# Weighted sums of the later pairs: both heads in one product over block-diagonal values, one transpose a pair

## The chip, the cores and the metric

The kernel runs on one core of one Trainium2 chip. The metric is device time of one execution in microseconds (us); lower is better. The median of three runs of the kernel before is 865.38 us (864.91 to 868.30).

## The reference

Sparse attention over 8 batches, 8 heads, 576 positions and head width 64, followed by a feed-forward layer with softplus, in 32-bit floats.

```python
scores = scale * np.matmul(q, k.transpose(0, 1, 3, 2))
mask_local = (rel >= 0) & (rel < stride)                                  # heads 0 to 3, stride 32
mask_strided = (rel >= 0) & (pos[None, :] % stride == pos[:, None] % stride)  # heads 4 to 7
attn = softmax(np.where(masks[None, :, :, :], scores, -1000000000.0))
out = np.matmul(attn, v)                         # (8, 8, 576, 64) -> x of 4608 x 512
h = x @ w_in                                     # w_in 512 x 2048
g = np.maximum(h, 0.0) + np.log1p(np.exp(-np.abs(h)))
return (g @ w_out).astype(np.float32)            # w_out 2048 x 512
```

(The softmax line is shortened; the reference writes out maximum, exponential and sum.)

## The kernel before

**Layout.** A *pair* is two heads of one batch; 32 pairs are numbered `n` = 0 to 31, four a batch. Positions of a pair are laid out in 18 blocks of 32 queries (strided heads are re-sorted on the host), and a block sees two blocks of 32 keys: the one before it and its own. For the pairs from 8 on (batch 3 on, 24 pairs), chunk `x` = 0 to 8 stands for two blocks, one in *place* 0 (blocks 0 to 8) and one in *place* 1 (blocks 9 to 17). A chunk's probabilities lie on 128 partitions, `64 * place + 32 * h` and up for head `h`, and in 64 columns, `c` = 0 for the earlier 32 keys and `c` = 1 for the own ones. In chunks 6 to 8 the two heads change places within a place (`place_of`).

**One pair from 8 on.** `head_scores` multiplies queries and keys (36 products of 64 rows and 32 columns, moving 64), VectorE adds the mask (`add_mask`), takes maxima, subtracts, ScalarE takes exponentials, VectorE sums and normalizes. Then `turn` transposes 32 by 32 blocks on VectorE in three tasks, `P{n}.0`, `P{n}.1` and `P{n}`: one whole transpose of 128 partitions and 576 columns (L550), then two transposes of 32 partitions by 288 columns that bring the own keys of the lower 32 partitions up (L555), and two that bring the earlier keys of the upper 32 partitions down (L557). After them the 64 keys of one head lie on the 64 partitions of a place. `late_sums` (L574) then multiplies: for each chunk, place and head one product of 64 rows (keys), 64 columns (the head's values) and 32 moving queries, into half the partitions of one of two PSUM banks, `po` for place 0 and `pv` for place 1. That is 36 products a pair. Each 32-bit product leaves two records of a weight load and two of a product in the trace, 72 a pair.

**Values.** `load_v` fetches `v_late`: on 64 partitions a place, the two key blocks of each chunk with both heads side by side (rows of 512 B). Each value is loaded twice. Three transfers a pair: 32 partitions for the first own block (L320) and 64 partitions a place (L329). For pair 8 GpSimd first zeroes 32 partitions (L318), the block before the first.

**The feed-forward part.** The rest is two kinds of large products, 128 by 128 by 512: `hidden` (L774) and `output` (L843), three products each for a split into a high and a low part, and in the later chunks `product` (L946). One takes its turn behind the other on TensorE, and between them stand, every three steps, the scores of pair `n + 1` and the sums of pair `n` as one task (`S{n+1}`, function `scores_of`). ScalarE and VectorE work out softplus and the splits between.

**What sets the order.** Everything up to the load of pair 8's values and the first products of chunk 1 follows the list `FIRST`, written by hand. After that `Plan` simulates engines with given costs and due times and emits tasks by their planned start; the three transposes of a pair stand in it with costs of 0.80, 0.95 and 0.95. The engines' queues keep the emitted order. Loads and stores are issued from SyncE (SP).

**Memory.** `home_0` to `home_3` are fixed tiles used piecewise: in `home_0` lie `v_late`, `qT` and `mask_late`; in `home_1` the probabilities, `turned` (the transposed ones) and, for pairs 4 to 7, their values `v_in`.

Of the kernel before, what the change touches and what calls it, by code (L numbers as in the profile page):

```python
# [11 lines left out]
BF16 = mybir.dt.bfloat16  # L12
# [6 lines left out]
P = 128  # L19
# [57 lines left out]
class Plan:  # L77
# [8 lines left out]
    def add(self, name, urgency, engine, cost, fn, after=(), late=0.0):  # L86
        self.tasks[name] = (urgency, len(self.tasks), engine, cost, fn, after, late)
# [29 lines left out]
def attention_softplus_ffn(  # L117
# [9 lines left out]
    nc = tc.nc  # L127
    B, NPAIR, _, _, S = qk.shape
    D = P // 2
# [6 lines left out]
    NCHK = NTILE * 3 // 2  # L136
# [30 lines left out]
    homes = [home(k, n, f"home_{k}") for k, n in enumerate(HOMES)]  # L167
# [39 lines left out]
        early[part, PAIRS[-1]][:, lo : lo + 4 * TILE].rearrange("p (h a c) -> p h a c", h=2, a=2)  # L207
        for part, lo in (("l", PAD + S), ("l", PAD + S + 4 * TILE), ("h", 2 * S))
    ]
    mask_late = homes[0][:, 3 * S : 3 * S + NCHK * 32].bitcast(BF16)  # L210
    v_late = homes[0][:, : 2 * S].rearrange("p (x d) -> p x d", d=2 * D)
    turned = homes[1][:, 2 * S : 3 * S].rearrange("p (c x l) -> p c x l", c=2, l=32)
    qT = homes[0][:, 2 * S : 3 * S]
    kT = [homes[2][:, i * (PAD + S) : (i + 1) * (PAD + S)] for i in range(2)]
    v_in = homes[1][:, 2 * S : 2 * S + 2 * NTILE * D]
    prob_all = homes[1][:, : 2 * S]
# [54 lines left out]
    def prob_of(n):  # L271
        if n < NPAIR:
            chunks = prob_early[n][:, PAD:].rearrange("p (a c) -> p a c", c=3 * PAD)
            return chunks[:, :, :64]
        return prob[n % 2]
# [38 lines left out]
    def load_v(n):  # L314
        b, pair = order[n]
        if n >= 2 * NPAIR:
            if n == 2 * NPAIR:
                nc.gpsimd.memset(v_late[:32, 0], 0.0)  # L318
            src = v[b, pair]
            nc.sync.dma_start(v_late[32:64, 0], src[:32])  # L320
            for place in range(2):
                lo = 1 - place
                keys = src[32 * (NCHK * place + lo - 1) :]
                keys = bass.AP(
                    tensor=keys.tensor,
                    offset=keys.offset,
                    ap=[[2 * D, 64], [32 * 2 * D, NCHK - lo], [1, 2 * D]],
                )
                nc.sync.dma_start(v_late[64 * place : 64 * place + 64, lo:], keys)  # L329
            return  # L330
        if n < NPAIR:

            t = room[n]
        else:
            t = v_in
        t = t[:, : 2 * NTILE * D].rearrange("p (a c) -> p a c", c=2 * D)
        src = v[b, pair]
        nc.sync.dma_start(t[PAD:P, 0], src[0:TILE])
        src = src[TILE - PAD : 2 * TILE]
        src = bass.AP(  # L340
            tensor=src.tensor,
            offset=src.offset,
            ap=[src.ap[0], [TILE * 2 * D, NTILE - 1], src.ap[1]],
        )
        nc.sync.dma_start(t[:, 1:NTILE], src)
        vs[n] = t.rearrange("p a (h d) -> p a h d", d=D)
# [52 lines left out]
        if n == 0:  # L399
            add(False)  # L400

    def place_of(part, h):

        return 1 - h if part == 1 else h

    def head_scores(n):

        taken.append(n)
        pss[n, 0] = ps_s.tile([P, 512], F32, tag="ps", name=f"ps_{n}")
        shared[n] = ps_o.tile([P, 512], F32, tag="po", name=f"po_{n}")  # L410
        pss[n, 1] = shared[n][:, S // 2 :]
        for x in range(6):
            for chunk in (x, x + 3) if x > 2 else (x,):
                part = chunk // 6
                for place in range(2):
                    a, i = block_at(chunk, place) if n < 2 * NPAIR else (3 * place, chunk)
                    c = TILE * a + 32 * i
                    for h in range(2):
                        to = 64 * place + 32 * place_of(part, h)
                        head = slice(64 * h, 64 * h + 64)  # L420
                        at = 64 * (chunk - SPLIT[part][0])
                        nc.tensor.matmul(  # L422
                            pss[n, part][to : to + 32, at : at + 64],
                            lhsT=qT[head, c : c + 32],
                            rhs=k_of(n)[head, c : c + 64],
                            start=True,
                            stop=True,
                        )
# [114 lines left out]
                            src[:, lo:hi, 32 * c : 32 * c + 32],  # L543
                        )

    def turn(n, step):

        src = prob_of(n).rearrange("p x (c l) -> p c x l", l=32)
        if step == 0:
            nc.vector.transpose(turned, src)  # L550
            return
        for place in range(2):
            lower, upper = (slice(at, at + 32) for at in (64 * place, 64 * place + 32))
            if step == 1:
                nc.vector.transpose(turned[upper, 0], src[lower, 1])  # L555
            else:
                nc.vector.transpose(turned[lower, 1], src[upper, 0])  # L557

    def late_sums(n, joint):

        if joint:
            to = [shared[n + 1], ps_h.tile([P, 512], F32, tag="ph", name=f"pv_{n}_1")]
        else:
            taken.append(n)
            to = [
                ps_o.tile([P, 512], F32, tag="po", name=f"pv_{n}_0"),
                ps_s.tile([P, 512], F32, tag="ps", name=f"pv_{n}_1"),
            ]
        pos[n, 0], pos[n, 1] = to
        for x in range(NCHK):  # L570
            for place in range(2):
                rows = slice(64 * place, 64 * place + 64)
                for h in range(2):
                    nc.tensor.matmul(  # L574
                        to[place][64 * h : 64 * h + 64, 32 * x : 32 * x + 32],
                        lhsT=v_late[rows, x, D * h : D * h + D],
                        rhs=turned[rows, place_of(x // 6, h), x],
                        start=True,
                        stop=True,
                    )  # L580

    def early_transposes(n, g):
# [128 lines left out]
    part = {}  # L711
# [474 lines left out]
    add = plan.add  # L1186
# [18 lines left out]
    for i in range(begin, len(steps)):  # L1205
        c, f = steps[i]
        w, x = CH[c] / 384, when[i]
        after = [f"F{i-1}", f"u{i-2}", f"G{c}.{f}"] + lows_of(c)
# [3 lines left out]
        after = [f"F{i}", f"Us{i-2}" if f"Us{i-2}" in plan.tasks else f"l{i-2}"]  # L1212
# [4 lines left out]
        else:  # L1217
            after = [f"u{i}", f"O{i-3}"]
            add(f"h{i}", x + 4.1, "ACT", 0.65, lambda c=c, f=f: g_high(c, f, nc.scalar), after)
            after = [f"h{i}", f"O{i-3}"]  # L1220
            fn = lambda c=c, f=f: g_low(c, f, nc.vector)
# [4 lines left out]
        c, f = steps[k]  # L1226
        w = CH[c] / 384
        x = when[i] + 2.1 * w
# [5 lines left out]
        for t in range(nt):  # L1234
            name = f"O{k}" if t == nt - 1 else f"O{k}.{t}"
            after = [f"l{k}", before] + ([f"y{k-1}.{t}"] if f == 0 else [])
            add(name, x + 0.01 * t, "PE", 0.7, lambda c=c, f=f, t=t: output(c, f, (t,)), after)
            before = name
            if f == NFC - 1:
                e, cost, engine = (("ACT", 0.5, nc.scalar), ("DVE", 0.6, nc.vector))[t % 2]  # L1240
                fn = lambda c=c, t=t, engine=engine: result(c, t, engine)
# [4 lines left out]
    for c in range(2, NEAR):  # L1246
        for f in range(10 if c > 2 else 12, NFC):
            old = NFC * c + f - 2 if f > 11 else NFC * (c - 1) + f + 4
            after = [f"F{old}", f"Wt{f}", f"Wt{f-2}"]
# [8 lines left out]
    def scores_of(n, x, y, name, e, cost, after, also=None):  # L1258

        z = x - 11.0  # L1260
        if n > 2 * NPAIR:
            add(f"Q{n}", z, "ACT", 1.4, lambda n=n: lay_out_q(n), [f"q{n}", f"S{n-1}"])

        def work():
            head_scores(n)
            if also is not None:
                sums_of(also)

        add(name, x, e, cost, work, after)
        for j in range(2):  # L1270
            fn = lambda j=j: add_mask(n, j)
            add(f"Y{n}{j}", y + j, "DVE", 0.47, fn, [f"S{n}", f"P{n-2}"])
        after = [f"Y{n}0", f"Y{n}1"]
        for j, (letter, e, cost, fn) in enumerate(
            (
                ("x", "DVE", 0.75, row_maxima),
                ("s", "DVE", 0.75, row_subtract),
                ("E", "ACT", 0.7, row_exp),
                ("z", "DVE", 0.75, row_sums),
                ("g", "DVE", 0.16, lambda n: guard(n, nc.vector)),  # L1280
                ("R", "DVE", 0.2, reciprocals),
                ("M", "DVE", 0.75, lambda n: normalize(n, nc.vector)),
            )
        ):
            add(f"{letter}{n}", y + 1.5 + j, e, cost, lambda fn=fn: fn(n), after)
            after = [f"{letter}{n}"]
        for j, (name, step, cost) in enumerate(
            ((f"P{n}.0", 0, 0.8), (f"P{n}.1", 1, 0.95), (f"P{n}", 2, 0.95))
        ):
            fn = lambda step=step: turn(n, step)  # L1290
            add(name, y + 8.5 + 0.9 * j, "DVE", cost, fn, after)
            after = [name]
        if n + 2 < len(order):
            add(f"k{n+2}", x + 5, "SP", 0.8, lambda: load_k(n + 2), [f"S{n}"], 2.0)
            add(f"q{n+2}", x + 18, "SP", 0.8, lambda: load_q(n + 2), [f"P{n}"], 2.0)
# [432 lines left out]
```

## Time and profile before

| what | value |
|---|---|
| median of three runs | 865.38 us |
| the profiled execution | 865.32 us |
| its span, first to last instruction | 863.5 us |
| granted TensorE clock | 1.000 |
| ScalarE busy | 494.2 us (57%) |
| GpSimd busy | 66.4 us (8%) |

The profile page lists busy time by engine, a row by slices of the span, the chain of work that ended last, and groups of instructions by line. PE is TensorE's products, PEld its weight loads, DVE is VectorE, ACT ScalarE, POOL GpSimd, and SPq SyncE's queue that issues DMAs. L574 is line 574 of the kernel. In a row of instructions, `64*64 64x32` is a product of 64 rows and 64 columns of weights with an output of 64 by 32. A timeline row begins with the start and the duration in us; a row with x2 merges neighbours, and its duration runs from the first start to the last end. The rows that carry the argument stand in the prediction.

### The profile page before, as it was taken

How to read it: one execution, taken by the hardware profiler on the slowest of the kernel's cores; microseconds unless marked ns; L12 is line 12 of the kernel's file. 1: busy time of each engine (PE TensorE's matmuls, PEld its weight loads, DVE VectorE, ACT ScalarE, POOL GpSimd, SP SyncE). 2: the span in 40 equal slices, each digit the busy share in tenths (PEclk: the TensorE clock that was granted, in tenths of full speed). 3: DMA queues.
4: the chain of work that ended last, by engine and by line, in shares of the span. 5: the costliest groups of instructions: out<-in, count | busy, mean ns of one | idle time of the engine just before them, and what ended most of it. 6: DMA issues, size and time to landing. Idle time of an engine off the chain costs nothing.

```text
span 863.5 us, 18656 instructions
## 1 busy us (share of the span) xinstructions
PE 853.9 (99%) x7688; PEld 703.3 (81%) x7688; DVE 584.3 (68%) x1106; ACT 494.2 (57%) x913; POOL 66.4 (8%) x89
## 2 busy tenths in 40 slices
PE   7999999999999999999999999999999999999998
PEld 5787888888888888888888888788888888888886
DVE  7899977677686668776668866666687645656500
ACT  6998755665555555646555655766664355566400
POOL 6345550000000000000000000000000000000000
PEclk9999999999999999999999999999999999999999
DMA  9894215556422554326424543655546144333100
GB/s 325 286 354 152 58 47 195 184 161 217 137 84 90 171 149 130 104 80 200 130 76 149 155 125 118 198 177 187 174 148 209 50 158 135 109 123 122 45 29 24
DMA packets 85332, 124.49 MB, mean 144 GB/s; under 512 B 7296, under 2 KB 52480, under 8 KB 85248
## 3 DMA queue, kind: packets, MB, share of 16 engines
q1 hardware_dynamic: 84960, 122.99, 43.8%
q8 instruction: 60, 0.98, 0.5%
q10 hardware_dynamic: 288, 0.33, 0.1%
q14 instruction: 24, 0.20, 0.1%
HBM read 92.88 MB, written 30.41 MB: 143 GB/s over the span
## 4 chain that ended last, share of the span: by engine, by line
PE 93%; DMA 2%; DVE 2%; ACT 1%; issue 1%; POOL 0%; SPq 0%; ACTq 0%; POOLq 0%
PE py L843 43%; PE ph L774 24%; PE bank_a L946 10%; PE bank_c L946 5%; PE po L574 2%; PE bank_b L946 2%; DMA ro<-in_moe_w_out_dram 2%; PE ps L422 2%; PE py_last L843 1%; PE po L422 1%; PE pv L574 1%; PE pv L640 1%; PE pt L610 1%; DVE home L536 1%; DMA raw_q<-in_qk_dram 0%
## 5 line engine op out<-in xcount | busy, mean ns | idle before, releaser
L843 PE MATMUL py<-w_o,gh 128*128 128x512 f32 x1024 | 318.3, 392 | 0.0
L843 PEld LDWEIGHTS py<-w_o,gh 128*128 128x128 f32 x1024 | 190.4, 188 | 39.5
L774 PE MATMUL ph<-x_h,w_i 128*128 128x512 f32 x656 | 202.7, 390 | 0.5 <-DVE u L798 0.5
L843 PE MATMUL py<-w_o,gl 128*128 128x512 f32 x512 | 199.2, 389 | 0.0
L774 PEld LDWEIGHTS ph<-x_h,w_i 128*128 128x128 f32 x656 | 122.5, 188 | 26.7 <-POOL home L525 0.9
L774 PE MATMUL ph<-x_l,w_i 128*128 128x512 f32 x328 | 127.6, 389 | 0.0
L843 PEld LDWEIGHTS py<-w_o,gl 128*128 128x128 f32 x512 | 96.1, 188 | 20.2
L290 ACT CAST gh<-u 128x512 fp32r<-128x512 f32 x89 | 55.1, 621 | 96.4 <-DVE u L798 74.5
L786 ACT ACTIVATE u<-ph 128x512 f32<-128x512 f32 x84 | 50.2, 599 | 94.8 <-PE ph L774 92.2
L828 DVE TENSOR_TENSOR gl<-u,gh 128x512 fp32r<-128x512 f32 x117 | 80.8, 691 | 25.0 <-ACT gh L290 21.9
L789 ACT ACTIVATE u<-u 128x512 f32<-128x512 f32 x144 | 90.9, 633 | 3.8
L791 ACT ACTIVATE u<-u 128x512 f32<-128x512 f32 x144 | 90.8, 631 | 3.7
L798 DVE SCALAR_TENSOR_TENSOR u<-ph,u 128x512 f32<-128x512 f32 x84 | 57.7, 687 | 37.3 <-ACT u L791 36.6
L774 PEld LDWEIGHTS ph<-x_l,w_i 128*128 128x128 f32 x328 | 61.6, 188 | 13.0
L786 ACT ACTIVATE u<-kept 128x512 f32<-128x512 f32 x45 | 28.5, 633 | 42.4 <-DVE kept L1042 26.0
L290 DVE COPY o<-py 128x512 f32<-128x512 f32 (+1 forms) x15 | 10.0, 670 | 47.0 <-PE py L843 46.8
L481 DVE TENSOR_TENSOR home<-ps,home 128x384 f32<-128x384 f32 x28 | 15.5, 555 | 36.4 <-PE ps L422 34.9
L1042 DVE TENSOR_TENSOR kept<-bank_c,kept 128x512 f32<-128x512 f32 x15 | 10.4, 692 | 36.5 <-PE bank_c L946 35.2
L290 ACT COPY home<-home 128x576 f32<-128x576 f32 x26 | 33.5, 1290 | 1.6 <-DMA home<-in_qk_dram 1.6
L290 ACT COPY o<-py 128x512 f32<-128x512 f32 (+1 forms) x21 | 11.5, 575 | 38.1 <-PE py L843 27.3
L1037 ACT COPY kept<-bank_a 128x512 f32<-128x512 f32 x30 | 17.7, 589 | 25.5 <-PE bank_a L946 24.5
L422 PEld LDWEIGHTS ps<-home,home 64*32 64x32 f32 x1344 | 23.3, 106 | 9.9 <-issue 8.1
(205 smaller groups left out, 1299.5 us busy)
## 6 DMA issues: line engine op xcount, KB each, us to landing
home<-in_qk_dram SPq DMA_DIRECT2D x56, 288.0 KB, 3.5
ws<-far SPq DMA_DIRECT2D x30, 512.0 KB, 3.3
out_dram<-o SPq DMA_DIRECT2D x35, 256.0 KB, 2.3
ri<-in_moe_w_in_dram SPq DMA_DIRECT2D x16, 512.0 KB, 7.3
ro<-in_moe_w_out_dram SPq DMA_DIRECT2D x16, 512.0 KB, 8.3
far_w<-w_i SPq DMA_DIRECT2D x16, 512.0 KB, 4.5
w_i<-far_w SPq DMA_DIRECT2D x16, 512.0 KB, 3.4
near<-far_w SPq DMA_DIRECT2D x15, 512.0 KB, 3.3
```

The lines of the kernel that those rows point to most:

```text
L290: (engine.copy if engine is nc.scalar else engine.tensor_copy)(dst, src)
L422: nc.tensor.matmul(pss[n, part][to : to + 32, at : at + 64], lhsT=qT[head, c : c + 32], rhs=k_of(n)[head, c : c + 64], start=True, stop=True,)
L574: nc.tensor.matmul(to[place][64 * h : 64 * h + 64, 32 * x : 32 * x + 32], lhsT=v_late[rows, x, D * h : D * h + D], rhs=turned[rows, place_ ...
L774: nc.tensor.matmul(ph, lhsT=w_i(c, f)[:, half, cc * P : (cc + 1) * P], rhs=x_at(x, cc, c), start=(i == 0), stop=(i == 3 * NCC - 1),)
L786: nc.scalar.activation(us[c, f], phs[c, f], AF.Abs)
L789: nc.scalar.activation(u, u, AF.Exp, scale=-1.0)
L791: nc.scalar.activation(u, u, AF.Ln, bias=1.0)
L798: nc.vector.scalar_tensor_tensor(to, in0=ph, scalar=0.0, in1=u, op0=ALU.max, op1=ALU.add)
L828: engine.tensor_tensor(g, us.pop((c, f)), ghs[c, f].bitcast(F32), op=ALU.subtract)
L843: nc.tensor.matmul(y_of(c, t), lhsT=g[:, sl], rhs=w32["o", f][:, half], start=(f == ROWS[c][0] and n == 0), stop=(f == ROWS[c][-1] and n = ...
L946: nc.tensor.matmul(bank, lhsT=w_left(p, A, f, half, i), rhs=x_right(p, A, part, i), start=p in "125" and n == 0, stop=n == 5, skip_group_c ...
L1037: nc.scalar.copy(kept(A, s), bank_of(p, A, f))
```

## The change

For the pairs from 8 on, the values are laid out block-diagonally. On the 32 partitions of a place and a head lie that head's values of one key block, in that head's 64 columns, and the other head's 64 columns hold zeros. `v_late` gets ten such blocks of 128 columns (a block more than there are chunks, since chunk `x` takes blocks `x` and `x + 1`). One whole transpose by 32 by 32 blocks leaves the keys `c` of both heads on a place's 64 partitions, and that is now what a product takes: 64 rows (32 keys of head 0, 32 of head 1), 128 columns (both heads), 32 moving queries, and two of them, `c` = 0 and 1, add up. So there are again 36 products a pair: 9 chunks, 2 key blocks, 2 places.

The four transposes of 32 partitions a pair are gone. The heads no longer change places in chunks 6 to 8 of these pairs. Values arrive in four transfers a pair (32 partitions, 9 or 10 rows of 256 B each) without the double copy. The zeros are written once, for pair 8: one fill of 64 partitions and four of 32 partitions by 640 columns. `v_late` grows from 1152 to 1280 columns, so `qT` moves up in `home_0` and `mask_late` moves to `home_1`.

```diff
-    mask_late = homes[0][:, 3 * S : 3 * S + NCHK * 32].bitcast(BF16)
-    v_late = homes[0][:, : 2 * S].rearrange("p (x d) -> p x d", d=2 * D)
+    mask_late = homes[1][:, 3 * S : 3 * S + NCHK * 32].bitcast(BF16)
+    v_late = homes[0][:, : (NCHK + 1) * 2 * D].rearrange("p (x h d) -> p x h d", h=2, d=D)
...
-    qT = homes[0][:, 2 * S : 3 * S]
+    qT = homes[0][:, (NCHK + 1) * 2 * D : (NCHK + 1) * 2 * D + S]
...
-                nc.gpsimd.memset(v_late[:32, 0], 0.0)
-            src = v[b, pair]
-            nc.sync.dma_start(v_late[32:64, 0], src[:32])
+                nc.gpsimd.memset(v_late[:64, 0], 0.0)
+                for quarter in range(4):
+                    rows = slice(32 * quarter, 32 * quarter + 32)
+                    nc.gpsimd.memset(v_late[rows, :, 1 - quarter % 2], 0.0)
+            src = v[b, pair].rearrange("(x l) (h d) -> l x h d", l=32, h=2)
             for place in range(2):
                 lo = 1 - place
...
-                nc.sync.dma_start(v_late[64 * place : 64 * place + 64, lo:], keys)
+                for h in range(2):
+                    rows = slice(64 * place + 32 * h, 64 * place + 32 * h + 32)
+                    keys = src[:, NCHK * place + lo - 1 : NCHK * place + NCHK, h]
+                    nc.sync.dma_start(v_late[rows, lo:, h], keys)
...
-        return 1 - h if part == 1 else h
+        return 1 - h if part == 1 and n < 2 * NPAIR else h
...
-        if step == 0:
-            nc.vector.transpose(turned, src)
-            return
-        for place in range(2):
-            lower, upper = (slice(at, at + 32) for at in (64 * place, 64 * place + 32))
-            if step == 1:
-                nc.vector.transpose(turned[upper, 0], src[lower, 1])
-            else:
-                nc.vector.transpose(turned[lower, 1], src[upper, 0])
+        nc.vector.transpose(turned, prob_of(n).rearrange("p x (c l) -> p c x l", l=32))
...
         for x in range(NCHK):
-            for place in range(2):
-                rows = slice(64 * place, 64 * place + 64)
-                for h in range(2):
+            for c in range(2):
+                for place in range(2):
+                    rows = slice(64 * place, 64 * place + 64)
                     nc.tensor.matmul(
-                        to[place][64 * h : 64 * h + 64, 32 * x : 32 * x + 32],
-                        lhsT=v_late[rows, x, D * h : D * h + D],
-                        rhs=turned[rows, place_of(x // 6, h), x],
-                        start=True,
-                        stop=True,
+                        to[place][:, 32 * x : 32 * x + 32],
+                        lhsT=v_late[rows, x + c].rearrange("p h d -> p (h d)"),
+                        rhs=turned[rows, c, x],
+                        start=c == 0,
+                        stop=c == 1,
                     )
...
-            ((f"P{n}.0", 0, 0.8), (f"P{n}.1", 1, 0.95), (f"P{n}", 2, 0.95))
...
+        add(f"P{n}", y + 8.5, "DVE", 0.8, lambda: turn(n), after)
```

The order of instructions shows what the planner makes of it. On TensorE, the end of the first sums (pair 8, behind the scores of pair 9) and the output products behind it stood like this before; `po_2013` and `pv_1_2050` are the two PSUM banks, `home_95` holds the transposed probabilities and `home_94` the values:

```order
L574 MATMUL po_2013<-home_95,home_94 64x32 x2
L574 MATMUL pv_1_2050<-home_95,home_94 64x32 x2
L843 MATMUL py_106<-w_o_948,gh_3_1963 128x512 x2
L843 MATMUL py_106<-w_o_948,gl_3_1965 128x512
L843 MATMUL py_107<-w_o_948,gh_3_1963 128x512 x2
L843 MATMUL py_107<-w_o_948,gl_3_1965 128x512
```

In the changed kernel (its own line numbers: 564 for the sums, 833 for the output) the same place reads:

```order
L564 MATMUL po_2023<-home_95,home_94 128x32
L564 MATMUL pv_1_2060<-home_95,home_94 128x32
L833 MATMUL py_106<-w_o_948,gh_3_1969 128x512 x2
L833 MATMUL py_106<-w_o_948,gl_3_1971 128x512
L833 MATMUL py_107<-w_o_948,gh_3_1969 128x512 x2
L833 MATMUL py_107<-w_o_948,gl_3_1971 128x512
```

Nothing else moves on TensorE in the whole program: the sums stand at the same 24 places, 36 products each, but two at a time in four array quarters have become one at a time in each half, 128 wide.

On VectorE, the end of pair 8 (normalizing, transposes) before, with softplus (`u`), the low part of a split (`gl`) and preparations for later weights (`ww`) around it:

```order
L525 TENSOR_TENSOR home_95<-home_95,st_1887 128x576
L550 STREAM_TRANSPOSE home_95<-home_95 128x576
L798 SCALAR_TENSOR_TENSOR u_3_1937<-ph_3_1906,u_3_1937 128x512
L555 STREAM_TRANSPOSE home_95<-home_95 32x288 x2
L828 TENSOR_TENSOR gl_3_1965<-u_3_1937,gh_3_1963 128x512
L557 STREAM_TRANSPOSE home_95<-home_95 32x288 x2
L994 TENSOR_TENSOR ww_4_1987<-w_i_1217 128x512
L1007 TENSOR_TENSOR ww_4_1987<-ww_4_1987 128x256
```

and in the changed kernel:

```order
L524 TENSOR_TENSOR home_95<-home_95,st_1892 128x576
L547 STREAM_TRANSPOSE home_95<-home_95 128x576
L788 SCALAR_TENSOR_TENSOR u_3_1942<-ph_3_1911,u_3_1942 128x512
L984 TENSOR_TENSOR ww_4_1967<-w_i_1217 128x512
L818 TENSOR_TENSOR gl_3_1971<-u_3_1942,gh_3_1969 128x512
L997 TENSOR_TENSOR ww_4_1967<-ww_4_1967 128x256
```

The two pairs of small transposes are out, and the weight preparations move into their place; later pairs look alike.

On GpSimd, the end of its program before, where `home_94` is filled with zeros for pair 8's values and `gl_15`, `w_o` are needed by the last output products of chunk 0:

```order
L743 TENSOR_TENSOR w_o_1720<-a_o_1492,w_o_1720 128x512
L318 MEMSET home_94 32x128
L828 TENSOR_TENSOR gl_15_1766<-u_15_1665,gh_15_1727 128x512
L743 TENSOR_TENSOR w_o_1759<-a_o_1617,w_o_1759 128x512
L290 COPY home_94<-home_95 128x576
```

and in the changed kernel:

```order
L733 TENSOR_TENSOR w_o_1720<-a_o_1492,w_o_1720 128x512
L318 MEMSET home_94 64x128
L321 MEMSET home_94 32x10x64 x4
L818 TENSOR_TENSOR gl_15_1771<-u_15_1665,gh_15_1727 128x512
L733 TENSOR_TENSOR w_o_1759<-a_o_1617,w_o_1759 128x512
L290 COPY home_94<-home_95 128x576
```

Four fills of 640 columns now stand ahead of the last three tasks.

More of the change, by code (lines that the diff above doesn't have):

```diff
@@ L317, in load_v @@
             if n == 2 * NPAIR:
-                nc.gpsimd.memset(v_late[:32, 0], 0.0)
-            src = v[b, pair]
-            nc.sync.dma_start(v_late[32:64, 0], src[:32])
+                nc.gpsimd.memset(v_late[:64, 0], 0.0)
[3 more added lines that the diff above has]
+            src = v[b, pair].rearrange("(x l) (h d) -> l x h d", l=32, h=2)
             for place in range(2):
                 lo = 1 - place
[L323 to L329, printed above, removed]
+                for h in range(2):
+                    rows = slice(64 * place + 32 * h, 64 * place + 32 * h + 32)
+                    keys = src[:, NCHK * place + lo - 1 : NCHK * place + NCHK, h]
+                    nc.sync.dma_start(v_late[rows, lo:, h], keys)
             return
@@ L400, in scores, with place_of @@
             add(False)
-    def place_of(part, h):
-        return 1 - h if part == 1 else h
+    def place_of(part, h, n=0):
+        return 1 - h if part == 1 and n < 2 * NPAIR else h
     def head_scores(n):
@@ L418, in head_scores @@
                     for h in range(2):
-                        to = 64 * place + 32 * place_of(part, h)
+                        to = 64 * place + 32 * place_of(part, h, n)
                         head = slice(64 * h, 64 * h + 64)
@@ L544, in prob_transposes, with turn @@
                         )
-    def turn(n, step):
-        src = prob_of(n).rearrange("p x (c l) -> p c x l", l=32)
-        if step == 0:
-            nc.vector.transpose(turned, src)
-            return
-        for place in range(2):
-            lower, upper = (slice(at, at + 32) for at in (64 * place, 64 * place + 32))
-            if step == 1:
-                nc.vector.transpose(turned[upper, 0], src[lower, 1])
-            else:
-                nc.vector.transpose(turned[lower, 1], src[upper, 0])
+    def turn(n):
+        nc.vector.transpose(turned, prob_of(n).rearrange("p x (c l) -> p c x l", l=32))
     def late_sums(n, joint):
@@ L1286, in scores_of @@
             after = [f"{letter}{n}"]
-        for j, (name, step, cost) in enumerate(
-            ((f"P{n}.0", 0, 0.8), (f"P{n}.1", 1, 0.95), (f"P{n}", 2, 0.95))
[L1289 to L1292, printed above, removed]
+        add(f"P{n}", y + 8.5, "DVE", 0.8, lambda: turn(n), after)
         if n + 2 < len(order):
```

## The prediction

> **What bounds the kernel now.** I read the page's row of engines first, then its chain of the work that ended last, then windows over the stretch in which all 24 changed pairs lie (the sums, L574, run from 152.1 to 671.6 us).
>
> ```profile
> PE 853.9 (99%) x7688; PEld 703.3 (81%) x7688; DVE 584.3 (68%) x1106; ACT 494.2 (57%) x913; POOL 66.4 (8%) x89
> PE 93%; DMA 2%; DVE 2%; ACT 1%; issue 1%; POOL 0%; SPq 0%; ACTq 0%; POOLq 0%
> 130.00:672.00 542.00, 541.89 (x5592) 447.44 (x5591) 382.99 (x712) 313.79 (x539) 0.00 (x0) 1.00 0.47 150
> 130.00:672.00 542.00, 30.04 (x1728) 27.38 (x1728) 1.00 0.47 150
> ```
>
> The last two rows are windows: length, then busy time (and records) of TensorE's products, its weight loads and, in the first of them, VectorE, ScalarE and GpSimd, then clock, DMA share and GB/s. The second row counts L574 alone. In 542 us TensorE's products leave 0.11 us uncovered. VectorE has 542 - 383 = 159 us to spare there. So a microsecond taken from VectorE buys nothing in this stretch, and a microsecond added to TensorE's queue is a microsecond of the kernel. The sums are part of that queue: 1728 records, 72 a pair. The question is how long the 72 records of a pair take when their weights are 128 columns wide.
>
> **What sets the pace of the sums.** The timeline of TensorE shows one pair's stretch. I quote its beginning and its end:
>
> ```profile
> 189.56 0.25 PE L574 MATMUL po<-home,home 64*64 64x32 f32 x2
> 189.57 0.25 PE L574 MATMUL pv<-home,home 64*64 64x32 f32 x2
> 189.64 0.23 PE L574 MATMUL po<-home,home 64*64 64x32 f32 x2
> 189.65 0.23 PE L574 MATMUL pv<-home,home 64*64 64x32 f32 x2
> 189.70 0.23 PE L574 MATMUL po<-home,home 64*64 64x32 f32 x2
> 189.71 0.23 PE L574 MATMUL pv<-home,home 64*64 64x32 f32 x2
> ...
> 190.57 0.23 PE L574 MATMUL po<-home,home 64*64 64x32 f32 x2
> 190.59 0.23 PE L574 MATMUL pv<-home,home 64*64 64x32 f32 x2
> 190.74 0.73 PE L843 MATMUL py<-w_o,gh 128*128 128x512 f32 x2
> ```
>
> Four records (two heads in `po`, two in `pv`) start within some 0.02 us, then nothing starts for about 0.04 us, then the next four. So the array works as four quarters side by side, each with 18 records a pair, and each quarter has a beat of its own: (190.57 - 189.64) / 16 = 58 ns. From the first record to the next product it is 190.74 - 189.56 = 1.18 us. Is the beat that of the streamed queries or of the weights? Other groups vary the two:
>
> ```profile
> L422 PEld LDWEIGHTS ps<-home,home 64*32 64x32 f32 x1344 | 23.3, 106 | 9.9 <-issue 8.1 <-ACT u L791 0.4 <-ACT u L789 0.4
> L574 PEld LDWEIGHTS pv<-home,home 64*64 64x64 f32 x936 | 27.1, 135 | 0.7 <-issue 0.4 <-PE py L843 0.4
> L843 PEld LDWEIGHTS py<-w_o,gh 128*128 128x128 f32 x1024 | 190.4, 188 | 39.5
> L610 PE MATMUL pt<-room,home 128*64 128x64 f32 x48 | 1.9, 222 | 0.0
> 25.20 0.64 PE L610 MATMUL pt<-room,home 128*64 128x64 f32 x16
> L640 PE MATMUL pv<-home,room 128*64 128x96 f32 x48 | 2.9, 246 | 0.0
> 24.65 0.67 PE L640 MATMUL pv<-home,room 128*64 128x96 f32 x12
> ```
>
> L610 and L640 load 64 columns, as the sums do, on two column halves side by side. L610 streams 64 elements: 16 records, 8 a half, take 0.64 us, less the 0.22 us of the last one, over 7 beats: 60 ns. L640 streams 96: (0.67 - 0.25) / 5 = 84 ns. A beat of 84 ns for 96 streamed elements is 0.9 ns an element, so the 32 of the sums would need 28 ns. They have 58, as much as the group with twice the stream and the same 64 columns. I take it that the weight load sets the beat of the sums. The load rows say what a column costs: 135 - 106 = 29 ns for 32 more, 188 - 135 = 53 ns for 64 more.
>
> **The change, part by part.**
>
> *The products.* Still 36 a pair and 72 records, but 128 columns wide: only two places, the row halves, are left to work side by side, with 36 records each instead of 18 in each of four quarters. The beat grows by the 64 columns: 58 + 53 = 111 ns. That the two row halves do overlap over the same columns the rows show: `pv` (the other 64 rows) starts 0.01 us behind `po`. A stretch is then 35 beats x 0.111 = 3.89 us from first to last start. Before it was 0.08 for the first beat and 0.93 for the 16 behind it, 1.01 us. I leave the 0.17 us behind the last start as it is (190.74 - 190.57), and put 0.05 us on the first load, which nothing covers. Growth: 3.89 - 1.01 + 0.05 = 2.93 us a pair, and 24 x 2.93 = **70.3 us**, all of it on TensorE's queue. Both ends of the price: if the beat stayed at 58 ns (a stream with a floor, the longer load hidden), 35 x 0.058 - 1.01 = 1.0 us a pair, +24 us. If the halves took turns, 71 x 0.111 - 1.01 = 6.9 us a pair, +165 us. I take the middle one since both the beats and the loads' rows give it.
>
> The Trainium skill, "TensorE: Matmul & The Clock Gate", section "LDWEIGHTS (loading the stationary operand)", has a load cost its columns divided by 1.2 ns, whatever the number of rows. By it the beat would be 107 ns, a stretch 3.73 us and the sum +67 us; the trace's 58 ns at 64 columns, where it has 53, is why I stay at 111.
>
> *The transposes.* Gone are two tasks of two a pair:
>
> ```profile
> L555 DVE STREAM_TRANSPOSE home<-home 32x288 f32<-32x288 f32 x48 | 22.5, 470 | 1.1
> L557 DVE STREAM_TRANSPOSE home<-home 32x288 f32<-32x288 f32 x48 | 22.5, 470 | 0.7
> ```
>
> That is 96 x 0.470 = 45 us of VectorE, 1.9 us a pair, and a shorter way from the normalized probabilities to the sums. It hides under TensorE today: with 0.11 us uncovered in 542, I book no gain. Nothing else was waiting that could come forward, since the order of the products on TensorE is the same. VectorE's own order shifts (weight preparations come earlier); with 159 us to spare I book nothing for that either.
>
> *The values.* Four transfers a pair for three. Bytes fall from 288 + 256 + 16 = 560 KB to 38 rows x 32 partitions x 256 B = 304 KB.
>
> ```profile
> L320 SPq DMA_DIRECT2D home<-in_v_dram x24: 327/382/1341, 121.7 to 645.0; - x24
> L329 SPq DMA_DIRECT2D home<-in_v_dram x48: 596/602/1602, 122.1 to 647.0; - x48
> home<-in_v_dram SPq DMA_DIRECT2D x24, 288.0 KB, 4.1
> ```
>
> Issuing took 0.38 + 2 x 0.60 = 1.58 us a pair; at the 0.60 of the nearest row it will be 2.4. Behind it in SP's queue stand the query and key loads and the weight stores. The values are issued after one pair's sums and needed at the next, 542 / 24 = 22.6 us on, and landed in 4.1 us: 18 us of cover, and 3 us more once the stretches are longer. I book nothing; if the 0.8 us reached TensorE each time it would be 20 us. The mask's transfer now writes where pairs 4 to 7 had their values, but it stands in SP's queue behind pair 8's values, which wait for those same last reads already.
>
> *The zeros.* Once, on GpSimd:
>
> ```profile
> 121.74 0.41 POOL L318 MEMSET home<- 32x128 f32 x1 [4.70 <-PE pv L640]
> 122.12 1.65 POOL L828 TENSOR_TENSOR gl<-u,gh 128x512 fp32r<-128x512 f32 x1
> 124.14 1.29 POOL L743 TENSOR_TENSOR w_o<-a_o,w_o 128x512 fp32r<-128x512 f32 x1 [0.36 <-DVE w_o L290]
> L251 POOL MEMSET early_h<- 64x576 f32 x4 | 2.3, 573 | 0.2
> 128.07 0.62 PE L843 MATMUL py<-w_o,gh 128*128 128x512 f32 x2
> ```
>
> Four fills of 640 columns at 573 ns for 576 are about 2.5 us. The low part of `w_o`, done at 125.43, comes at about 128.0 instead, and the second product of the row at 128.07 (0.23 us later) reads it. It just fits; I book 0, and up to 0.5 us if not.
>
> **The sum.** The profiled execution took 865.32 us, 1.8 us more than its span of 863.5, and stands 0.06 us under the median of 865.38. 863.5 + 70.3 + 1.8 = 935.6; I forecast **935.6 us**.
>
> **Rivals.**
>
> *The beat does not grow* (0.06). If 58 ns is a floor of short streams and a second weight load runs ahead unseen, only the loss of two quarters counts: +24 us, 889 us. For it: no row here has 128 columns with a short stream. Against it: then L610's 64 elements would have to sit on that same floor by chance, and 53 ns for 64 more columns would have to vanish.
>
> *Not slower: a shared pace* (0.04). If all 72 records passed one gate at 1.03 / 72 = 14 ns each, however wide they are, the same 72 would take the same 1.18 us, and the 0.11 us of idle time is all that VectorE's relief could bring: 865 us. The point where it decides is a beat of 29 ns in each half; each 10 ns above that cost 35 x 24 x 0.01 = 8.4 us. Against it: the starts come in bunches of four with a hole behind, not evenly.
> The Trainium skill, on the same page under "Back-to-back issue gap", speaks against a loss in this way: start to start never falls below about 25 ns however short the stream. By that, 72 records would need 1.8 us before and after alike. The trace disagrees, with 72 starts in 1.03 us.
>
> *The halves take turns* (0.05). If a product over all columns keeps the other row half waiting, it is +165 us, 1030 us. Against it: the quarters share columns today and overlap.
>
> **Chances and range.** The forecast has 0.85. Its own spread: a beat of 104 to 120 ns gives 35 x 24 x (-0.007 to +0.009) = -6 to +8 us, and small stalls -1 to +3. The range of 927 to 947 holds that and leaves out the rivals and a little more, 2 in 10. About 0.5% (4.3 us) is what a measurement of this kernel can tell from no change: slower by more has 0.95, within it 0.04, faster 0.01, since even the whole idle time before 152 us would not pay for more.
>
> **What would show each step.** In the profile after: the sums' records as 64 rows and 128 columns, starts in bunches of two, 0.11 us apart; loads of about 188 ns; a stretch of 4.1 us from the first record of the sums to the next product; busy time of the sums near 24 x 4.1 = 99 us; VectorE down by 45 us; TensorE still without idle time between 130 us and the last pair. Wrong would be a beat of 58 ns (first rival), of 29 (second), single starts 0.11 us apart (third). A clock under 1.00 within the sums, which this execution shows nowhere, would break the forecast upward.

## The result, and the profile after

The changed kernel takes 968.34 us (median of four runs, 966.84 to 970.89) where the kernel before takes 865.28 beside it: a ratio of 1.119, 95% interval 1.115 to 1.122. The forecast was 935.6 us, with a range up to 947. So the direction was right, and a third of the loss was not foreseen: +103 us measured, +70 forecast.

First the page of the changed kernel: its row of engines and its chain. In its line numbers L564 are the sums, L833 the output products and L421 the scores.

```profile
PE 956.4 (99%) x7688; PEld 798.6 (83%) x7688; DVE 539.9 (56%) x1010; ACT 493.9 (51%) x913; POOL 68.6 (7%) x93
PE py L833 41%; PE ph L764 21%; PE po L564 9%; PE bank_a L936 9%; PE bank_c L936 4%; PE bank_b L936 2%; PE ps L421 2%; DMA ro<-in_moe_w_out_dram 2%; PE pv L564 1%; PE py_last L833 1%; PE po L421 1%; PE pv L630 1%; DVE home L535 0%; PE pt L600 0%; DMA raw_q<-in_qk_dram 0%
```

Then windows over the stretch that holds the changed pairs (length, busy time and records of TensorE's products, weight loads, VectorE, ScalarE, GpSimd, then clock, DMA share, GB/s), and the same window for the sums alone:

```profile
130.00:775.00 645.00, 644.89 (x5591) 542.69 (x5590) 340.40 (x622) 313.62 (x539) 0.00 (x0) 0.95 0.37 117
130.00:775.00 645.00, 102.86 (x1728) 100.06 (x1728) 0.95 0.37 117
```

TensorE is as gapless as before (0.11 us uncovered), VectorE has lost 44 us of work, and the sums' busy time has gone from 30 to 103 us. The new thing is the clock, 0.95 on average over this stretch. Three places show where the time went.

**The sums.** TensorE's timeline, one pair, its beginning and its end:

```profile
176.25 0.29 PE L564 MATMUL po<-home,home 64*128 64x32 f32 x1
176.26 0.29 PE L564 MATMUL pv<-home,home 64*128 64x32 f32 x1
176.39 0.27 PE L564 MATMUL po<-home,home 64*128 64x32 f32 x1
176.39 0.27 PE L564 MATMUL pv<-home,home 64*128 64x32 f32 x1
176.50 0.27 PE L564 MATMUL po<-home,home 64*128 64x32 f32 x1
...
180.18 0.27 PE L564 MATMUL po<-home,home 64*128 64x32 f32 x1
180.19 0.27 PE L564 MATMUL pv<-home,home 64*128 64x32 f32 x1
180.39 0.73 PE L833 MATMUL py<-w_o,gh 128*128 128x512 f32 x2
```

And the group of its weight loads (busy us, mean ns of one):

```profile
L564 PEld LDWEIGHTS po<-home,home 64*128 64x128 f32 x792 | 91.5, 190 | 2.0
```

A load is as long as those of the large products. Starts come in twos, (180.18 - 176.39) / 34 = 111 ns apart, and a stretch lasts 180.39 - 176.25 = 4.14 us where it lasted 1.18. That is 2.96 us more, 24 x 2.96 = 71.0 us.

**The clock.** Windows with the granted clock (the column behind the engines), cut along the changes of the trace's clock record: the sums of a later pair, the 3.41 us behind, and the 6 us behind those:

```profile
198.07:202.07 4.00, 4.00 (x79) 4.00 (x72) 0.56 (x1) 0.86 (x2) 0.00 (x0) 1.00 0.30 78
202.07:205.48 3.41, 3.41 (x12) 2.67 (x11) 2.66 (x7) 2.15 (x5) 0.00 (x0) 0.50 0.46 114
205.48:211.48 6.00, 6.00 (x28) 4.94 (x27) 3.78 (x7) 2.93 (x5) 0.00 (x0) 1.00 0.55 185
```

Output products at the half clock, from TensorE's timeline:

```profile
203.74 1.05 PE L833 MATMUL py<-w_o,gh 128*128 128x512 f32 x2
204.59 0.63 PE L833 MATMUL py<-w_o,gl 128*128 128x512 f32 x1
205.02 0.85 PE L833 MATMUL py<-w_o,gh 128*128 128x512 f32 x2
```

TensorE never stands idle here, yet its clock goes to half right behind the sums. Three large products take 205.02 - 203.74 = 1.28 us, 427 ns each. At full clock, right behind that span, three take 206.63 - 205.94 = 0.69 us; over the whole trace the median distance of two starts at full clock is 227 ns:

```profile
205.94 0.62 PE L833 MATMUL py<-w_o,gh 128*128 128x512 f32 x2
206.40 0.39 PE L833 MATMUL py<-w_o,gl 128*128 128x512 f32 x1
206.63 0.62 PE L764 MATMUL ph<-x_h,w_i 128*128 128x512 f32 x2
```

The clock record holds 17 such spans, 16 of 3.41 us and one of 6.83, 61.4 us in all (and one at the very end, as before). If all of it fell on large products it would cost 61.4 x (1 - 227/427) = 28.8 us. Counted in the trace, 134 large products start within the 17 spans, and at 200 ns more for each they cost 26.8 us.

**The scores.** TensorE's timeline, the scores of a pair from their first to their last group: before, then after.

```profile
188.57 0.48 PE L422 MATMUL ps<-home,home 64*32 64x64 f32 x20
...
189.36 0.27 PE L422 MATMUL po<-home,home 64*32 64x64 f32 x4
```

```profile
175.12 0.65 PE L421 MATMUL ps<-home,home 64*32 64x64 f32 x32
...
176.03 0.29 PE L421 MATMUL po<-home,home 64*32 64x64 f32 x8
```

Before, the sums followed at 189.56, 0.99 us behind the scores' first record; after, they follow at 176.25, 1.13 us behind. The trace has 0.989 us for every pair before, and 1.139 for each of the 24 pairs after: 24 x 0.150 = 3.6 us.

The profiled spans differ by 965.7 - 863.5 = 102.2 us: 71.0 for the sums, 3.6 for the scores, and 27.6 left, which lies between the two prices of the spans at half clock.

### The profile page after: what moved, and what is told of

Its sections match the earlier page's. It is cut to its first block, busy times and chain, and to the rows that moved or that the text cites. A ratio compares the mean times of both kernels' runs of the same rounds, so it can differ in the third digit from the quotient of the medians.

```text
span 965.7 us, 18596 instructions
## 1 busy us (share of the span) xinstructions
PE 956.4 (99%) x7688; PEld 798.6 (83%) x7688; DVE 539.9 (56%) x1010; ACT 493.9 (51%) x913; POOL 68.6 (7%) x93
## 4 chain that ended last, share of the span: by engine, by line
PE 93%; DMA 2%; DVE 2%; ACT 1%; issue 1%; POOL 0%; SPq 0%; ACTq 0%; POOLq 0%
PE py L833 41%; PE ph L764 21%; PE po L564 9%; PE bank_a L936 9%; PE bank_c L936 4%; PE bank_b L936 2%; PE ps L421 2%; DMA ro<-in_moe_w_out_dram 2%; PE pv L564 1%; PE py_last L833 1%; PE po L421 1%; PE pv L630 1%; DVE home L535 0%; PE pt L600 0%; DMA raw_q<-in_qk_dram 0%
## 5 line engine op out<-in xcount | busy, mean ns | idle before, releaser
L833 PE MATMUL py<-w_o,gh 128*128 128x512 f32 x1024 | 336.1, 411 | 0.0
L833 PEld LDWEIGHTS py<-w_o,gh 128*128 128x128 f32 x1024 | 201.8, 199 | 43.7
L833 PE MATMUL py<-w_o,gl 128*128 128x512 f32 x512 | 207.7, 406 | 0.0
L833 PEld LDWEIGHTS py<-w_o,gl 128*128 128x128 f32 x512 | 101.7, 199 | 22.4
L564 PE MATMUL pv<-home,home 64*128 64x32 f32 x936 | 102.7, 276 | 0.0
L564 PEld LDWEIGHTS pv<-home,home 64*128 64x128 f32 x936 | 99.9, 190 | 0.7 <-issue 0.4
L564 PE MATMUL po<-home,home 64*128 64x32 f32 x792 | 94.1, 276 | 0.0
L564 PEld LDWEIGHTS po<-home,home 64*128 64x128 f32 x792 | 91.5, 190 | 2.0
L480 DVE TENSOR_TENSOR home<-po,home 128x192 f32<-128x192 f32 x28 | 9.9, 355 | 88.0 <-ACT x_h L681 71.4
L681 ACT CAST x_h<-po 128x288 fp32r<-128x288 f32 (+7 forms) x30 | 9.5, 334 | 63.6 <-PE pv L564 62.9
```

Of the source, the lines that this page charges most:

```text
L480: nc.vector.tensor_tensor(pv, sv, m, op=ALU.add)
L564: nc.tensor.matmul(to[place][:, 32 * x : 32 * x + 32], lhsT=v_late[rows, x + c].rearrange("p h d -> p (h d)"), rhs=turned[rows, c, x], sta ...
L833: nc.tensor.matmul(y_of(c, t), lhsT=g[:, sl], rhs=w32["o", f][:, half], start=(f == ROWS[c][0] and n == 0), stop=(f == ROWS[c][-1] and n = ...
```

## The experiments

The kernel before ran beside each group: 864.56 us in the first, 864.44 in the second. All ratios are to these.

**The heads in products of their own.** Is it the width that sets the beat?

```diff
-                        to[place][:, 32 * x : 32 * x + 32],
-                        lhsT=v_late[rows, x + c].rearrange("p h d -> p (h d)"),
+                    for h in range(2):
...
+                            to[place][64 * h : 64 * h + 64, 32 * x : 32 * x + 32],
+                            lhsT=v_late[rows, x + c, h],
```

> The changed kernel, with each product of 128 columns taken as two of 64 columns, one a head (72 products, 144 records a pair, four quarters of the array, 36 records each). Theory (the weight load of a product's columns sets the beat of the part of the array it uses): the beat is back to 58 ns, a stretch takes 35 x 0.058 + 0.02 = 2.1 us from first to last start instead of 3.94, that is 1.0 us more than before in each of 24 pairs, +25 us on 865 = 890 us; at 2.1 us of sums on end the clock should stay at 1.00. Rival 1 (each record costs the same, whatever its width: 3.94 us / 72 = 55 ns): 144 records take 7.9 us, about 1060 us. Rival 2 (the new layout or its transfers cost the time, not the width of the products): 968 us, as with the change.

Measured: 923.74 us, 1.069 (1.067 to 1.071), which is none of the three. The timeline of TensorE has both what the theory left out (the first row, idle time in brackets) and its beat:

```profile
155.40 0.24 PE L565 MATMUL pv<-home,home 64*64 64x32 f32 x2 [2.02 <-issue]
...
196.55 0.23 PE L565 MATMUL po<-home,home 64*64 64x32 f32 x2
196.57 0.23 PE L565 MATMUL pv<-home,home 64*64 64x32 f32 x2
196.61 0.23 PE L565 MATMUL po<-home,home 64*64 64x32 f32 x2
```

The view of TensorE's waits (us in total, times, longest) puts them down to nothing that the profile shows:

```profile
PE pv L565 <- issue: 9.3, 6, 2.4
PE po L565 <- issue: 7.8, 5, 2.7
```

The beat is 58 ns again, and 13 of the 24 stretches have 2.08 us from first to last start, as expected. The other 11 have one hole each, of 1.1 to 3.0 us. Holes inside and behind the stretches sum to some 21.5 us, five spans at half clock cost some 8, the scores 3.6, and the longer stretches 24 x (2.23 - 1.18) = 25: 58 of the 59 us. Width and beat are confirmed on the unbroken stretches. The holes lie 256 records of TensorE (weight loads, products and waits counted alike) or a multiple of it apart, to within one. The page's row of instruction transfers goes from 60 packets before to 74 here:

```profile
q8 instruction: 60, 0.98, 0.5%
q8 instruction: 74, 1.21, 0.5%
```

A packet is 16384 B. The packets' times in the trace tie the two together: each of the 13 holes ends 1.2 to 1.6 us after the end of one such packet, whether that packet ended before the hole began or within it. The 34 holes of the run with the old sums four times, below, end 1.0 to 1.6 us after one. So TensorE waits for instructions there. That it is the density of short products which outpaces the supply is argued from this; it was not tested by itself. The Trainium skill, "Runtime: NRT & Kernel Launch", section "Instruction fetch mechanics", has instructions arrive in blocks of 16 KiB, 256 to a block, and the cost of a block's end mostly hidden. The distance of the holes agrees; the 21.5 us say that here it isn't hidden.

**The sums in two pieces.** Is it the unbroken stretch that brings the clock down?

```diff
-                sums_of(also)
+                late_sums(also, True, range(5) if n in i_of else range(9))
...
+            if joint(i) and t == 1:
+                n = pair_at[i] - 1
+                before = f"U{n}"
+                add(before, x + 0.015, "PE", 1.0, lambda n=n: late_sums(n, True, range(5, 9)), [name])
```

The second piece stands behind two of the four token tiles of the output products that followed the sums anyway.

> The changed kernel, with the sums of 19 of the 24 pairs in two pieces (5 chunks, then 4) and six of the output products that follow anyway put between them (1.4 us of large products). The products, loads and transfers are the same. Theory (of the 102 us that the change adds, 71 are longer beats, and some 31 come from 3.4 us at half clock behind most sums, because the sums fill 2.6 us or more of such a span): no half clock is left in the 19 pairs; each half-clock span cost about 3.4 x (1 - 227/427) = 1.6 us, 15 to 16 of them lie there, so about -26 us, and two more changes of the array's layout a pair at about 0.3 us cost +6: 945 to 950 us, mean clock 0.99 or more. Rival 1 (the clock falls because of the amount of such work in all, or a limit that has nothing to do with where the sums stand): still clock 0.968 and 968 to 974 us. Rival 2 (clock as in the theory, but the values or banks come late in the shorter gap): clock up, time still above 955.

Measured: 953.19 us, 1.102 (1.101 to 1.104), mean clock 0.991. Windows over the part with split sums and over the rest, where five pairs kept theirs in one piece:

```profile
130.00:560.00 430.00, 430.00 (x4210) 360.22 (x4209) 233.87 (x439) 205.08 (x359) 0.00 (x0) 1.00 0.35 110
570.00:775.00 205.00, 204.90 (x1399) 170.93 (x1398) 111.07 (x190) 104.40 (x180) 0.00 (x0) 0.96 0.42 133
```

With the same products, not one span at half clock is left where the sums are split; all four (17 us) lie behind the five unsplit ones. That fells the view that the amount of such work matters. The time is 3 us above the expected band, because I counted 15 or 16 spans as gone where 13 went (18 lengths of 3.41 us in the changed kernel, 5 here). By parts, the split stretches with their second entries come to 19 x 3.28 = 62 us over before, the five whole ones to 15, the half clock to 8 and the scores to 3.6: 89 us, against 88.6 measured.

**Twice the stream.** What is it in the sums that the clock goes by?

```diff
-                        to[place][:, 32 * x : 32 * x + 32],
+                        to[place][:, 32 * y : 32 * y + 64],      # y = min(x, 7)
...
-                        rhs=turned[rows, c, x],
+                        rhs=turned[rows, c, y : y + 2],
```

> The changed kernel, with each product of the sums moving 64 columns instead of 32 (the queries of two neighbouring chunks, so the sums are not those of the reference). Same number of products, same weights. Theory (the load of 128 columns sets the beat): 36 beats of 112 ns a half as with the change, the stretch stays at 3.94 us where the clock is full. Rival (the stream sets the beat): 64 streamed elements take longer than 32, a beat of some 140 to 220 ns and 990 us or more. On the clock there are two views. If what counts is how much the array streams, the doubled stream (53 of 112 ns instead of 27) should leave fewer half-clock spans or none, and the time goes to 937 to 950 us; if it is the small products as such, the clock stays at 0.968 and the time at 968 us.

Measured: 940.54 us, 1.089 (1.087 to 1.090), clock 1.000. The timeline of the sums:

```profile
195.45 0.27 PE L565 MATMUL pv<-home,home 64*128 64x64 f32 x1
195.56 0.27 PE L565 MATMUL po<-home,home 64*128 64x64 f32 x1
195.67 0.27 PE L565 MATMUL po<-home,home 64*128 64x64 f32 x1
```

and a window over all of them:

```profile
130.00:760.00 630.00, 629.89 (x5648) 532.55 (x5647) 347.84 (x634) 318.20 (x547) 0.00 (x0) 1.00 0.39 121
```

The beat stays at 111 ns with twice the stream, so the stream doesn't set it, and the time of the changed kernel falls by 28 us because no span at half clock is left before the end. Same number of records, same loads, a stretch of nearly the same length (4.165 us for 4.14): what differs is how much the array streams. The rest, 940.5 - 864.6 = 76.0 us, is the sums (24 x 2.98 = 71.6) and the scores (3.6), to within 0.8 us.

**The old sums four times.** Meant to show whether any 4 us of small products bring the clock down.

```diff
-        for x in range(NCHK):
+        for x in [x for _ in range(4) for x in range(NCHK)]:
```

> The kernel before, with the products of each pair's sums issued four times over (the same values each time). 72 beats of 58 ns in each quarter, 4.2 us on end, as long as the changed kernel's sums. The growth by beats alone is 3 x 18 x 0.058 x 24 = 75 us, 941 us. If the clock falls because the array sits in small products for over 2.6 us, whatever they are, half-clock spans appear as with the change and the time goes to 968 to 975 us with a mean clock near 0.97. If it falls because only 36 records of 32 streamed elements a half pass in 3.9 us, four quarters at a beat of 58 ns have four times as many starts in the same time, the clock stays at 1.00 and the time at 941 us.

Measured: 1063.71 us, 1.231 (1.225 to 1.237), clock 0.928. It doesn't answer the question, since the sums are full of holes of the kind above. The view of the sums' line has the idle time before its instructions (us, times):

```profile
its engine sat idle before it (us, times) until:
  issue: 119.0, 70
```

(The 119 us count weight loads and products both; between starts on TensorE the holes sum to 65 us.) Every stretch has at least one hole, the longest of 4.3 us, so half clock may come from the holes as well as from the products. Nor does the number of starts decide it here: of seven spans of 3.41 us with 128 starts of the sums each, five are followed by half clock and two are not. What stays open is whether four busy quarters with a beat of 58 ns would keep the clock up for 4 us.

**VectorE's relief alone.** The kernel before without the small transposes (a `return` behind the first one).

> The kernel before without the four small transposes a pair (L555, L557), so the sums read blocks that were not brought together. Theory (VectorE's relief is worth nothing where TensorE's products leave 0.11 us of 542 uncovered): VectorE about 45 us less busy, time 864 to 866 us, within 0.2% of before. Rival (the shorter way from probabilities to sums takes waits off TensorE): 860 us or less.

Measured: 864.46 us, 1.000 (0.9988 to 1.0012), with VectorE at 539.1 us for 584.3. Worth nothing, as expected.

**The swap of heads alone.** The kernel before, with only this (and the number of the pair handed to it):

```diff
-        return 1 - h if part == 1 else h
+        return 1 - h if part == 1 and n < 2 * NPAIR else h
```

> The kernel before with one line's part of the change alone: in the pairs from 8 on the heads no longer change places in chunks 6 to 8, in scores and sums alike. In the trace of the changed kernel the scores of these pairs took 1.139 us from first record to the next product where they took 0.989 before. Theory (with the swap, chunk x and chunk x + 3 write other quarters of the columns and overlap; without it they share them and one waits for the other): 24 x 0.15 = 3.6 us more, 868 to 869 us. Rival (the longer scores come from the moved queries or another part of the change): 864.6 us, and scores of 0.99 us.

Measured: 869.30 us, 1.0059 (1.0046 to 1.0071). Scores and the sums behind them:

```profile
169.26 0.65 PE L422 MATMUL ps<-home,home 64*32 64x64 f32 x32
...
170.18 0.29 PE L422 MATMUL po<-home,home 64*32 64x64 f32 x8
170.40 0.25 PE L574 MATMUL po<-home,home 64*64 64x32 f32 x2
```

170.40 - 169.26 = 1.14 us: the longer scores are this edit's doing. The starts fit the theory: without the swap four records start every 36 ns to the end, the last at 0.99 us; with it they come closer together from 0.32 us on, the last at 0.84. The edit cost 4.9 us rather than 3.6. Some 1.0 us of the rest is visible: the first dozen output products behind each sums start a few ns later each, 0.04 us a pair. Why, is open.

**The change with narrow products.** All of the change but the width.

```diff
-                        to[place][:, 32 * x : 32 * x + 32],
-                        lhsT=v_late[rows, x + c].rearrange("p h d -> p (h d)"),
+                        to[place][64 * c : 64 * c + 64, 32 * x : 32 * x + 32],
+                        lhsT=v_late[rows, x + c, c],
```

> The changed kernel with 64 instead of 128 columns a product: the first key block gives head 0 alone, the second head 1 alone (half of each head's keys are left out of the sums). 36 products and 72 records a pair as in the changed kernel, in four quarters again, all else as changed: layout, transfers, zeros, transposes, scores without the swap. Theory (width sets the beat, and nothing else of the change costs anything but the scores' 3.6 us): beat 58 ns, stretches of 1.18 us, clock 1.00, 868 to 869.5 us. Rival (transfers of 256 B rows, a fourth issue a pair or the zeros cost some us that the long stretches hide in the changed kernel): 871 us or more.

Measured: 869.67 us, 1.0058 (1.0045 to 1.0071), clock 1.000. A window over the sums alone shows them at their old 30 us:

```profile
130.00:680.00 550.00, 30.04 (x1728) 27.38 (x1728) 1.00 0.44 137
```

The time is the swap's price within 0.4 us, though a little above the band. Transfers, zeros and the block-diagonal layout together cost nothing that these runs can tell (the interval is some 1 us either way). None of the kernels is faster than the one before.

## Why the prediction failed, step by step

- **The bound** was read rightly. TensorE's products left 0.11 us uncovered before and after, and the 45 us taken from VectorE bought nothing (864.46 beside 864.44 us).
- **The beat** was right in kind and size: 111 ns forecast and measured, a stretch of 4.14 us for 4.1, +71.0 us for +70.3. Twice the stream left it unchanged, half the width brought 58 ns back. The three rivals (beat of 58 ns, a shared pace, halves in turn) all fell with the pairs of starts 111 ns apart.
- **Values and zeros** at nothing: right, by the kernel with narrow products. A transfer of values landed in 2.2 us; the zeros took 2.8 us where I estimated 2.5, and no wait of TensorE came of them. From GpSimd's timeline of the changed kernel, and from its DMA issues:

```profile
120.99 2.81 POOL L321 MEMSET home<- 32x640 f32 x4
```

```profile
home<-in_v_dram SPq DMA_DIRECT2D x48, 80.0 KB, 2.2
```

- **The failed step** is the one from the sums to the whole: "Growth: ... 24 x 2.93 = 70.3 us, all of it on TensorE's queue", with "small stalls -1 to +3" for all else. It took the rest of the queue to keep its pace. In its place the runs showed 17 spans at half clock behind the sums, 27.6 us, which were gone where the sums were split or streamed twice as much. I had named a clock under 1.00 as what would break the forecast, and then neither priced it nor gave it a chance; the only ground on record is that the clock was 1.00 throughout before. But no row of before had more than 1.18 us of sums on end, so that was no evidence about 4 us. A span at half clock cost 3.41 x (1 - 227/427) = 1.6 us; one behind each of the 24 pairs would be 38 us, and the range should have reached to 974.
- **The missed edit**: "the order of the products on TensorE is the same" was true and was taken for "their time is the same". The scores' targets had moved: with the heads swapped in chunks 6 to 8, chunk x and chunk x + 3 wrote different quarters of the columns and overlapped. Without the swap they share them. 3.6 us in the trace, 4.9 alone in a kernel.

When does the clock fall? In the changed kernel's clock record all its changes lie 3.41 us or a multiple of it apart. Cut into such lengths, every span of 3.41 us at full clock with 2.59 us or more of sums is followed by half clock, and none with 2.50 or less is. So of 24 stretches 17 met it and 7 lay too evenly across a boundary. (In the run with the sums in two pieces, one of the five whole stretches brought it down with 2.56 us.) The Trainium skill, "TensorE: Matmul & The Clock Gate", section "The HAM clock gate (the "warmup" mystery)", has a free-running window of 3413 ns and a clock that halves after an idle one. The window agrees. Idle in the sense of nothing to do it was not: in the window of 198.07 to 202.07 us TensorE is busy for 4.00 us of 4.00, and the clock halves at its end. What fits these runs is a count of what the array streams, since doubling the stream was enough to keep the clock; how the chip counts it is open.

## What to carry to other kernels

For a product with a short stream, count the weight columns that each part of the array must load one behind the other, not products: 36 products of 64 columns in four quarters took 1.18 us, 36 of 128 columns in two halves 4.14. Before lengthening a run of short-stream products, lay its length beside the clock's windows (here 3.41 us) and price a span at half clock, even where the clock so far reads 1.00; if it must be long, break it with large products. And where an edit changes which partitions a product writes, look at which other products it used to overlap with, though the order stays word for word.

## What was unexpected of the hardware

- The clock went to half behind spans of 3.41 us with 2.6 us or more of products of 64 rows and 128 columns that stream 32 elements each 111 ns, with no idle time; with 64 elements it stayed at 1.00.
- Twice the records in the same 24 places brought holes of 0.9 to 3.0 us, 21.5 us in all, 256 records of TensorE or a multiple apart. No semaphore wait stands behind them, but each ends 1.2 to 1.6 us after a 16384 B packet of instructions.
- Records for four quarters of the array started 7 ns apart within a bunch, 72 in 1.03 us.
